# Block 0's x in two parts, conv weights decoded in PSUM, and new engine letters for the first blocks of a fused dynamic convolution and gated FFN

## The chip, the cores and the metric

One core of a Trainium2 chip runs the kernel. The metric is the device time of one execution in microseconds; lower is better. The engines are PE (matrix multiply), DVE (VectorE), ACT (ScalarE), POOL (GpSimd) and SP (which here only issues transfers). Each works through its own queue in order and waits for the others by semaphores.

## What is computed

Two layers, one after the other, on 4 sequences of 4160 tokens with 192 channels. The first is a dynamic convolution: per token and head (8 heads of 24 channels) a softmax over 7 weights, and the weighted sum of the last 7 rows of x. The second is a feed-forward layer with a convolution of width 3 over time as its gate.

```python
w = softmax(weight_gen)                     # over 7 taps, per token and head
out[s] = sum_k w[s, h, k] * x[s - 6 + k]    # rows before the sequence are zero
h = np.maximum(out @ w_in, 0.0)             # 192 -> 1024
conv_out[s] = sum_k conv_w[k] * h[s - 1 + k]
y = (h * sigmoid(conv_out)) @ w_out         # 1024 -> 192
```

## The kernel before

**Tiling.** The 16640 tokens are cut into 128 segments of 130 tokens, one per partition. A block is 4 tokens of every segment, so 512 tokens; with two rows of overlap there are 33 blocks. x lives in a ring of 24 rows per partition (`ring`). Block 0 also needs a halo, the seven rows in front of each segment: these are loaded from the neighbour's segment.

**Attention of block q** (`head`). Seven taps, one for each k (`tap`, L292), each multiply 4 rows of x with their softmax weights into a piece of `px` or `py`, 128 x 768 elements. A letter in `PLAN` says for each tap whether VectorE ("V") or GpSimd ("G") does it. Blocks 0 to 2 are of kind "a": PE adds the seven pieces while it transposes them (L327), in two parts of 128 and 64 channels, into the PSUM banks `tp` and `ops`; that is 14 groups of four transposes. Later blocks add most pieces by accumulating DMAs first. ACT and DVE then split the transposed sum into high and low float32r parts (L338, L343).

**Softmax of group j** (`sm_ops`, one group for block 0, then one for two blocks). Maximum (L239), subtract (L242), exponential on ACT (L245), sum (L248), a small constant (L252, L254), reciprocal (L257), normalise (L264) and, in the first rows of a sequence, an edge product that zeroes taps (L269). The letters in `SMX` say who does the subtract, and who the last two.

**FFN of block j** (`unit`, `out_tiles`). For each of the 8 slices f of 128 hidden channels PE runs five matmuls into one of 5 PSUM banks z (`mm1`, L359); ACT does the relu (L365) and the middle conv tap (L369), DVE the two outer ones (L376), ACT the tanh (L383), DVE the gate product (`gmul`, L392), which frees the bank. Then PE makes four output tiles (`mm2`, L405), ACT copies them out (L414) and SP stores them. A unit needs its weight slice (`w_rdy`), a bank and the split block.

**Weight decoding** (`dec`). All weights arrive as raw words and are decoded in six steps: on ACT the exponent shift (L133) and the low half (L136), then clamp (L140), shift (L143), sign (L146) and join (L151). In mode "S" the work lies in SBUF: the letters say who clamps and joins, shift and sign are DVE's. In mode "P" it lies in the single PSUM bank `dps`, all four steps are DVE's whatever the letters say, and the chunks follow each other through that bank. A chunk of w_in then gets a high part (ACT, L595) and a low part (L600). `CH` lists the chunks: "m" for channels 0 to 127, "f" for the other 64 folded in two, whose parts are then spread by DMA (L614). The conv weights are decoded by the same steps, transposed by PE (L567) into the `tp` bank and copied to `cw` by ACT (L572); the first transposes of block 0 on `tp`, and all relus of block 0, wait for that copy.

**Order.** The kernel lists all work as tasks with engine, estimated duration and dependences, places them by a list scheduler, and emits each engine's queue in that order. The list is ranked by `now`: softmaxes of the first groups and weight decoding first (-9), attention of block q at q + `TO`, its transposes at q + `FO`, the units of block j at j to j + 7/8, in block 0 in the order `FORD`, its output tiles from j + `WO_` on. `arrive(t)` stands for data expected at t. A task of kind "VK" is DVE work that the scheduler lets hold POOL too; before the next POOL task after one it emits a pair of memsets on a small tile, `tok` (L874 on DVE, L875 on POOL), so POOL waits there until DVE has got that far. In the other direction nothing is enforced.

**Loads.** SP issues, in this order: the fold chunk 0:256 (two transfers), x rows 0 to 2, the halo (112 and 15 partitions), weights of group 1, x of blocks 1 and 2, the other chunks of w_in, weights of groups 2 and 3. ACT issues the weights of group 0, the chunk m 0:256 and the conv weights.

## Time and profile before

| | us |
|---|---|
| median of 3 runs | 713.72 (713.22 to 714.27) |
| profiled execution, time | 713.11 |
| its span in the profile | 711.40 |
| PE busy | 690.1 (97%) |
| DVE busy | 625.6 (88%) |
| ACT busy | 549.9 (77%) |
| POOL busy | 510.5 (72%) |

The span runs from the first instruction to the last; 1.7 us of the time lie around it. Busy time is the union of the spans of an engine's instructions; the ends of matmuls are modelled. The share over the whole span hides the stages: nearly all of PE's idle time lies in the first 29 us and in the last 3 us.

### The profile page before, as it was taken

Reading aid. Unit: us, or ns where it says so; the run is one execution under the profiler, and the core shown is the slowest. Engines: PE = TensorE matmul, PEld = TensorE weight load, DVE = VectorE, ACT = ScalarE, POOL = GpSimd, SP = SyncE. Lnnn points to the kernel's source line nnn. Section 1 sums busy time; section 2 is a strip of 40 time slices with the busy share of each in tenths; the row PEclk is TensorE's granted clock in tenths of the full one; section 3 lists DMA queues with packets and bytes.
Section 4 is the critical chain, followed back from the end, with each engine's and each line's share of the span. In section 5 each row is a group of like instructions: output and inputs, shape, how many; then the busy total and the mean of one; then the engine's idle time right before and its main releaser. Section 6 shows DMA issues by size and latency. Waiting matters only on the chain.

```text
span 711.4 us, 10938 instructions
## 1 busy us (share of the span) xinstructions
PE 690.1 (97%) x3809; PEld 629.0 (88%) x3809; DVE 625.6 (88%) x975; ACT 549.9 (77%) x1049; POOL 510.5 (72%) x392
## 2 busy tenths in 40 slices
PE   1899999999999999999999999999999999999998
PEld 1788999999999999999999999999999999999998
DVE  6999998989999998998898988988898888888981
ACT  2588888887888787878787877878778778787881
POOL 3998999999987778887777778877767788630000
PEclk9999999999999999999999999999999999999999
DMA  7736999898989688798888788788879886781211
GB/s 226 212 98 166 215 217 225 211 236 197 229 186 211 166 208 200 167 209 189 193 193 200 190 181 202 184 200 193 188 181 200 178 183 163 163 181 68 76 43 45
DMA packets 70787, 127.59 MB, mean 179 GB/s; under 512 B 5046, under 2 KB 42573, under 8 KB 70732
## 3 DMA queue, kind: packets, MB, share of 16 engines
q0 software_dynamic: 20160, 58.99, 46.9%
q1 hardware_dynamic: 50090, 67.51, 29.3%
q8 instruction: 30, 0.49, 0.3%
q10 hardware_dynamic: 482, 0.40, 0.2%
q14 instruction: 25, 0.20, 0.1%
HBM read 20.51 MB, written 12.78 MB: 47 GB/s over the span
## 4 chain that ended last, share of the span: by engine, by line
PE 96%; DMA 2%; DVE 1%; POOL 0%; SPq 0%; ACT 0%; issue 0%; POOLq 0%
PE ops L405 47%; PE z L359 43%; PE tp L327 5%; DMA ring<-in_x_dram 1%; PE ops L327 1%; PE z L405 1%; DMA stage<-in_moe_w_in_dram 1%; DVE py L292 0%; POOL px L292 0%; POOL py L292 0%; SPq L437 0%; DVE r L257 0%; DVE m L248 0%; DVE w L242 0%; DVE px L292 0%
## 5 line engine op out<-in xcount | busy, mean ns | idle before, releaser
L376 DVE SCALAR_TENSOR_TENSOR z<-h,cw,z 128x512 f32<-128x512 f32 (+1 forms) x528 | 379.3, 741 | 25.7 <-ACT z L369 21.3
L405 PE MATMUL ops<-wo,g 128*128 128x192 f32 x2048 | 353.1, 326 | 0.0
L405 PEld LDWEIGHTS ops<-wo,g 128*128 128x128 f32 x2048 | 338.9, 190 | 10.0
L359 PE MATMUL z<-H,wi 128*128 128x512 f32 x1056 | 303.6, 409 | 1.0 <-ACT wi L595 1.0
L292 POOL TENSOR_TENSOR px<-ring,w 128x768 f32<-128x768 f32 (+2 forms) x146 | 231.9, 1702 | 79.6 <-PE tp L327 75.3
L359 PEld LDWEIGHTS z<-H,wi 128*128 128x128 f32 x1056 | 191.1, 189 | 32.5 <-ACT wi L595 1.4
L392 DVE SCALAR_TENSOR_TENSOR g<-z,h 128x512 f32<-128x512 f32 (+1 forms) x264 | 178.3, 679 | 22.3 <-ACT z L383 14.6
L383 ACT ACTIVATE z<-z 128x512 f32<-128x512 f32 (+1 forms) x264 | 151.3, 573 | 45.2 <-DVE z L376 43.4
L369 ACT ACTIVATE z<-h,cw 128x512 f32<-128x512 f32 (+1 forms) x264 | 179.9, 682 | 5.7
L365 ACT ACTIVATE h<-z 128x512 f32<-128x512 f32 x264 | 155.7, 590 | 29.1 <-PE z L359 27.8
L292 POOL TENSOR_TENSOR py<-ring,w 128x768 f32<-128x768 f32 (+2 forms) x108 | 162.8, 1813 | 2.2 <-DMA px<-py 2.2
L359 PE MATMUL z<-L,wi 128*128 128x512 f32 x264 | 103.1, 391 | 0.0
L322 POOL TENSOR_TENSOR px<-px 128x768 f32<-128x768 f32 x30 | 68.0, 2265 | 6.1 <-DMA px<-px 6.1
L414 ACT ACTIVATE o<-ops 128x192 f32<-128x192 f32 x128 | 41.9, 328 | 24.0 <-PE ops L405 22.8
L359 PEld LDWEIGHTS z<-L,wi 128*128 128x128 f32 x264 | 49.6, 188 | 11.2
L338 ACT ACTIVATE H<-tp 128x512 fp32r<-128x512 f32 (+1 forms) x63 | 37.3, 593 | 21.5 <-PE tp L327 20.1
L327 PE MATMUL tp<-ident,px 128*128 128x128 f32 (+1 forms) x288 | 44.5, 279 | 2.7 <-POOL px L292 1.9
L315 POOL DMA_DIRECT2D px<-py x30 | 41.3, 1377 | 7.2 <-POOL py L292 7.2
L318 POOL DMA_DIRECT2D px<-px x30 | 36.3, 1211 | 13.2 <-DMA px<-py 12.0
L327 PEld LDWEIGHTS tp<-ident,px 128*128 128x128 f32 (+1 forms) x288 | 34.6, 132 | 9.5 <-POOL px L292 2.4
L343 DVE TENSOR_TENSOR L<-tp,H 128x512 fp32r<-128x512 f32 x33 | 22.7, 687 | 6.9 <-ACT H L338 6.9
L343 DVE TENSOR_TENSOR H<-tp,H 64x512 fp32r<-64x512 f32 x30 | 20.5, 684 | 6.7 <-ACT H L338 5.9
(67 smaller groups left out, 180.4 us busy)
## 6 DMA issues: line engine op xcount, KB each, us to landing
px<-py POOLq DMA_DIRECT2D x30, 1152.0 KB, 10.2
h<-h SPq DMA_DIRECT2D x128, 256.0 KB, 4.4
px<-px POOLq DMA_DIRECT2D x30, 768.0 KB, 6.6
ring<-in_x_dram SPq DMA_DIRECT2D x31, 384.0 KB, 6.0
out_dram<-o SPq DMA_DIRECT2D x31, 384.0 KB, 2.4
w<-in_weight_gen_dram SPq DMA_DIRECT2D x15, 224.0 KB, 6.5
r_out<-in_moe_w_out_dram SPq DMA_DIRECT2D x4, 384.0 KB, 5.6
wi<-scr SPq DMA_DIRECT2D x8, 128.0 KB, 5.2
```

Source lines behind the costliest of these rows:

```text
L292: eng.tensor_tensor(out=dst[:, a:b, :].rearrange("p s (h g) -> p s h g", g=GRP), in0=ring[:, p:p + n, :].rearrange("p s (h g) -> p s h g", ...
L322: nc.gpsimd.tensor_tensor(out=a, in0=a, in1=b, op=ALU.add)
L327: nc.tensor.matmul(dst[0:D2 if part else P, c * P:(c + 1) * P], lhsT=src[:, c, part * P:part * D2 + P], rhs=ident, is_transpose=True, star ...
L343: nc.vector.tensor_tensor(out=H[D2:P, :] if part else h_t[q, "L1"], in0=tp[r, :], in1=H[r, :].bitcast(F32), op=ALU.subtract)
L359: nc.tensor.matmul(out=z, lhsT=w[:, fs], rhs=h_t[j, nm], start=(i == 0), stop=(i == len(terms) - 1))
L365: nc.scalar.activation(out=hrow(f, 2, R), in_=z_t[j, f], func=ACTF.Relu)
L369: nc.scalar.activation(out=z_t[j, f][:, :no * P], in_=hrow(f, cc, no), func=ACTF.Copy, scale=cw[:, NF + f:NF + f + 1])
L376: nc.vector.scalar_tensor_tensor(out=z, in0=hrow(f, cc + d, no), scalar=cw[:, k * NF + f:k * NF + f + 1], in1=z, op0=ALU.mult, op1=ALU.add,)
L383: nc.scalar.activation(out=z, in_=z, func=ACTF.Tanh, scale=0.5)
L392: nc.vector.scalar_tensor_tensor(out=g_of(j, f), in0=z_t[j, f][:, :no * P], scalar=1.0, in1=hrow(f, cc, no), op0=ALU.add, op1=ALU.mult)
L405: nc.tensor.matmul(out=ps[:, 0:D], lhsT=g_of(j, f)[:, i * P:(i + 1) * P], rhs=wo[:, f, :], start=(f == 0), stop=(f == NF - 1),)
L414: nc.scalar.activation(out=o_t[j][:, i, :], in_=ps[:, 0:D], func=ACTF.Copy, scale=0.5)
```

## The change

- `load_x` no longer loads the halo. A new `load_halo` does, called twice: rows -4 to -1 before x rows 0 to 2, and rows -7 to -5 after them. The zeroing of the first segment's halo stays ahead of both.
- `TORD`: block 0's taps are made, and added by PE, in the order 6, 5, 4, 3, 2, 1, 0; taps 3 to 6 of block 0 depend on the first part of x alone (expected at 8.6), the others on all of it (10.3). Later blocks keep their order.
- The conv weights are decoded in mode "P", and that work is listed behind the first two chunks of w_in; their expected arrival is 10.5 instead of 8.9.
- Engines: block 1's tap 2 goes to DVE. Group 0's subtract, normalise and edge product go from DVE to POOL; group 1's normalise and edge product go to POOL; group 2's subtract goes to DVE. The chunk m 256:512 is decoded in mode "S" with the clamp on POOL.
- The expected arrival of chunk m 0:256 becomes 10.4 (8.7); `TO`, `FO` and `WO_` are -2.55, -0.5 and 1.42; `FORD` is changed; the mask product of the last group goes from DVE to ACT.

```diff
 PLAN = (
     ("a", "GVGGVGG"),
-    ("a", "GGGGGGG"),
+    ("a", "GGVGGGG"),
     ("a", "GGGGGGG"),
 )
-SMX = ("VV", "VV", "GG", "GG")
+SMX = ("GG", "VG", "VG", "GG")
-TO = -2.7
-FO = -0.35
-WO_ = 1.62
+TO = -2.55
+FO = -0.5
+WO_ = 1.42
+TORD = ((6, 5, 4, 3, 2, 1, 0), (0, 1, 2, 4, 5, 6, 3))
 CH = (
     ("f", 0, 256, 5.2, "VGP", "G"),
-    ("m", 0, 256, 8.7, "VVP", "G"),
+    ("m", 0, 256, 10.4, "GVP", "V"),
     ("f", 256, 512, 17.0, "GVP", "V"),
-    ("m", 256, 512, 16.0, "VVP", "G"),
-    ("m", 512, 1024, 18.0, "VVP", "V"),
+    ("m", 256, 512, 16.0, "GVS", "V"),
+    ("m", 512, 1024, 18.0, "VVP", "G"),
 )
-FORD = (0, 3, 1, 5, 2, 4, 7, 6)
+FORD = (0, 2, 1, 3, 5, 4, 7, 6)
-WOE = ("VVP", "VVP", "GVP", "VGP")
+WOE = ("VVP", "VGP", "GGP", "VGP")
...
+    def load_halo(r0, r1):
+        p = slot(r0)
+        for p0, np_ in ((16, 112), (1, 15)):
+            nc.sync.dma_start(
+                out=ring[p0:p0 + np_, p:p + r1 - r0, :].rearrange("p s d -> p (s d)"),
+                in_=seg(xf, D, p0, np_, r0, r1 - r0),
+            )
...
         def keep():
             r = m(1)[:, (n - 1) * HEADS:, :]
-            V.tensor_scalar(out=r, in0=r, scalar1=mask[:, 1:2], scalar2=None, op0=ALU.mult)
+            nc.scalar.activation(out=r, in_=r, func=ACTF.Copy, scale=mask[:, 1:2])
...
-        load_x(-TAPS, 3)
+        G.memset(ring[0:1, slot(-TAPS):slot(0), :], 0.0)
+        load_halo(-4, 0)
+        load_x(0, 3)
+        load_halo(-TAPS, -4)
...
-        x_t_ = {0: arrive(10.3), 1: arrive(13.5), 2: arrive(15.0)}
+        x_t_ = {-1: arrive(8.6), 0: arrive(10.3), 1: arrive(13.5), 2: arrive(15.0)}
...
-        c0 = dec(cw_raw.bitcast(I32), r_cw, temps[0][0:3 * NF, 0:P], temps[1][0:3 * NF, 0:P], arrive(8.9), [], "VVS")[0]
+        def conv_weights():
+            banks = {}
+            c0 = dec(cw_raw.bitcast(I32), r_cw, temps[0][0:3 * NF, 0:P], temps[1][0:3 * NF, 0:P], arrive(10.5), [], "VVP")[0]
...
         for c, (kind, a, b, t, eng, wle) in enumerate(CH):
+            if c == 2:
+                c2 = conv_weights()
...
-            for i, k in ((0, 0), (1, 1), (2, 2), (4, 4), (5, 5), (6, 6), (3, 3)):
+            for i in TORD[q > 0]:
+                k = i
...
-                p_ = task("VK" if e == "V" else e, d_, [sm[group(q)], x_t_[q]] + (xdep if i < 4 else ydep),
+                p_ = task("VK" if e == "V" else e, d_, [sm[group(q)], x_t_[q if q or k < 3 else -1]] + (xdep if i < 4 else ydep),
...
-                out_ = [(i, prod[i]) for i in (0, 1, 2, 4, 5, 6, 3)]
+                out_ = [(i, prod[i]) for i in TORD[q > 0]]
```

## Rows read from the trace of the kernel before

**Rows 1.** Busy time by stage: stretch, length, busy of each engine, clock, DMA
```profile
14.36:28.93 14.57, 10.84 (x63) 9.05 (x64) 13.17 (x28) 5.28 (x14) 10.93 (x12) 1.00 0.66 171
28.93:56.97 28.04, 28.03 (x176) 23.90 (x176) 27.74 (x59) 24.70 (x51) 27.72 (x20) 1.00 0.44 146
85.20:105.61 20.41, 20.41 (x113) 18.72 (x113) 20.02 (x31) 16.99 (x33) 19.00 (x15) 1.00 0.93 213
123.44:143.89 20.45, 20.45 (x113) 18.68 (x113) 19.76 (x31) 16.68 (x32) 18.59 (x14) 1.00 0.92 212
```

**Rows 2.** Chain of work, issues (start, length), landings (last column), SP's wait
```profile
2.10 7.00 DMA ring<-in_x_dram
...
2.72 0.44 SPq L174 DMA_DIRECT2D ring<-in_x_dram  x1
...
ring<-in_x_dram SPq DMA_DIRECT2D x1, 588.0 KB, 7.6
...
2.60 0.36 ACTq L434 DMA_DIRECT2D stage<-in_moe_w_in_dram  x1
...
stage<-in_moe_w_in_dram ACTq DMA_DIRECT2D x1, 256.0 KB, 6.7
...
SPq L199 <- DMA ring<-in_x_dram: 3.6, 1, 3.6
```

**Rows 3.** DVE in order of time: start, length, line, operation, idle before
```profile
7.79 0.35 DVE L257 RECIPROCAL r<-m 128x32 f32<-128x32 f32 x1
...
10.88 0.21 DVE L140 TENSOR_SCALAR h<-h 24x128 f32<-24x128 f32 x1 [2.04 <-ACT h L133]
11.03 0.37 DVE L269 TENSOR_TENSOR w<-w,edge 128x224 f32<-128x224 f32 x1
...
13.03 1.18 DVE L151 CUSTOM_DVE_ANT_0 h<-h 24x256 uint16<-24x256 uint16 x1
...
15.35 1.02 DVE L242 TENSOR_TENSOR w<-w,m 128x448 f32<-128x448 f32 x1
16.30 0.94 DVE L292 TENSOR_TENSOR px<-ring,w 128x768 f32<-128x768 f32 x1
...
18.56 1.70 DVE L292 TENSOR_TENSOR py<-ring,w 128x768 f32<-128x768 f32 x1
20.19 0.61 DVE L264 TENSOR_TENSOR w<-w,r 128x448 f32<-128x448 f32 x1
...
21.99 0.67 DVE L269 TENSOR_TENSOR w<-w,edge 128x168 f32<-128x168 f32 x1
...
24.36 0.43 DVE L140 TENSOR_SCALAR dps<-dps 128x256 f32<-128x256 f32 x1 [0.47 <-ACT dps L133]
```

**Rows 4.** POOL in order of time, same columns
```profile
12.53 1.54 POOL L292 TENSOR_TENSOR px<-ring,w 128x768 f32<-128x768 f32 x1
...
17.85 0.10 POOL L875 MEMSET tok<- 128x1 f32 x1 [1.96 <-DVE tok L874]
...
20.87 0.10 POOL L875 MEMSET tok<- 128x1 f32 x1 [1.42 <-DVE tok L874]
...
22.79 1.54 POOL L292 TENSOR_TENSOR px<-ring,w 128x768 f32<-128x768 f32 x1
24.28 0.97 POOL L242 TENSOR_TENSOR w<-w,m 128x448 f32<-128x448 f32 x1
```

**Rows 5.** ACT in order of time, the fold chunk 256:512
```profile
17.97 0.39 ACT L133 ACTIVATE dps<-stage 128x256 f32<-128x256 f32 x1
```

**Rows 6.** End of the ramp: PE and DVE in order of time; PE's wait
```profile
50.90 0.55 DVE L151 CUSTOM_DVE_ANT_0 wo<-dps,scr 128x768 uint16<-128x768 uint16 x1
...
56.97 1.21 PE L359 MATMUL z<-H,wi 128*128 128x512 f32 x4
...
59.41 5.36 PE L405 MATMUL ops<-wo,g 128*128 128x192 f32 x32
...
PEld z L359 <- DVE g L392: 0.3, 1, 0.3
```

More of the change, by code (lines that the diff above doesn't have):

```diff
@@ L162, in slot @@
         return (r + TAPS + 2) % RING
+    def load_halo(r0, r1):
[5 more added lines that the diff above has]
+            )
     def load_x(r0, r1):
-        a, b = max(r0, 0), min(r1, SEG)
+        a, b = r0, min(r1, SEG)
         p = slot(a)
-        if r0 < 0:
-            nc.gpsimd.memset(ring[0:1, slot(r0):p, :], 0.0)
         nc.sync.dma_start(
@@ L171, in load_x @@
         )
-        if r0 < 0:
-            for p0, np_ in ((16, 112), (1, 15)):
-                nc.sync.dma_start(
-                    out=ring[p0:p0 + np_, slot(r0):p, :].rearrange("p s d -> p (s d)"),
-                    in_=seg(xf, D, p0, np_, r0, -r0),
-                )
         if r1 > SEG:
@@ L275, in sm_ops @@
              ("A" if j else "VK", 0.16 if j else 0.1, eps), ("V", 0.07 + 0.05 * n, rec)]
-            + ([("VK", 0.1, keep)] if j == NG - 1 else [])
+            + ([("A", 0.2, keep)] if j == NG - 1 else [])
             + [(ek[1], ed[1], norm)]
@@ L540, in bits @@
                     if 0 not in hold:
-                        hold[0] = ps_d.tile([P, W], F32, tag="dps", name="dps").bitcast(I32)[:, 0:N]
+                        hold[0] = ps_d.tile([P, W], F32, tag="dps", name="dps").bitcast(I32)[0:t1.shape[0], 0:N]
                     return hold[0]
@@ L561, in dec, with cw_fin @@
             return task("VK" if je == "V" else "G", vec(N, 0) if je == "V" else pool(N), [t_, i1], st[5]), bits
-        c0 = dec(cw_raw.bitcast(I32), r_cw, temps[0][0:3 * NF, 0:P], temps[1][0:3 * NF, 0:P], arrive(8.9), [], "VVS")[0]
-        def cw_fin():
-            cp = ps_t.tile([P, 4 * P], F32, tag="tp", name="tp")
-            nc.tensor.transpose(cp[:, 0:3 * NF], cw_raw, ident[0:3 * NF, 0:3 * NF])
-            banks["cw"] = cp
-        banks = {}
-        c1 = task("P", 0.1, [c0], cw_fin)
-        c2 = task("A", 0.1, [c1], lambda: nc.scalar.activation(out=cw, in_=banks["cw"][:, 0:3 * NF], func=ACTF.Copy))
+        def conv_weights():
+            banks = {}
+            c0 = dec(cw_raw.bitcast(I32), r_cw, temps[0][0:3 * NF, 0:P], temps[1][0:3 * NF, 0:P], arrive(10.5), [], "VVP")[0]
+            def cw_fin():
+                cp = ps_t.tile([P, 4 * P], F32, tag="tp", name="tp")
+                nc.tensor.transpose(cp[:, 0:3 * NF], cw_raw, ident[0:3 * NF, 0:3 * NF])
+                banks["cw"] = cp
+            c1 = task("P", 0.1, [c0], cw_fin)
+            return task("A", 0.1, [c1], lambda: nc.scalar.activation(out=cw, in_=banks["cw"][:, 0:3 * NF], func=ACTF.Copy))
         spreads = []
```

## The prediction, made before the change was run

> **What bounds the kernel now.** I read the busy time by stage first, then the waits of the matmul engine, then the first 60 us in order of time. From 28.93 us on PE has no idle time: 28.03 of 28.04 us up to 56.97, and 20.45 of 20.45 us in a block of the middle, at a granted clock of 1.00 [rows 1]. Such a block asks PE for 8 units of mm1 (L359), 4 output tiles (L405) and 2 transposes. So the end is fixed by when the dense stretch of PE begins, plus work that the change leaves as it is. Before 28.93 PE is busy 10.84 of 14.57 us, and before 14.36 not at all. What the change can win lies here; its reordering of the later blocks can win or lose only a little.
>
> What holds PE back until 28.93 is block 0: its seven taps feed the transposes, these the split, and this the first mm1. The first tap starts on POOL at 12.53 and the last POOL tap at 22.79 [rows 4], ending at 24.33; from there to 28.93 is 4.6 us of transposes, splits and the first unit. The five POOL taps last 5 x 1.54 = 7.7 us of the 11.8 us from 12.53 to 24.33. The other 4.1 us are token waits for VectorE, the longest 1.96 and 1.42 us [rows 4]. The start at 12.53 is late for a reason that is easy to miss: DVE had the reciprocals of group 0 at 8.14 and then stood still 2.04 us, because the first convolution-weight operation (L140 on h) was next in its queue and its data had not arrived; the edge product that frees the first tap (L269) stood behind it and started at 11.03 [rows 3].
>
> From 28.93 to 56.97 DVE is nearly as full as PE, 27.74 of 28.04 us [rows 1], and at 56.97 a unit of mm1 starts just after a wait of 0.3 us for a z bank that DVE had to free [rows 6]. So DVE is a second bound in the ramp, and a head start of PE is kept only as far as DVE follows or PE has something else to do.
>
> **First tap.** Two edits act on it. The conv-weight decode moves behind the decode of the main weights, so nothing late stands in front of group 0 on DVE; and subtract, normalise and edge product of group 0 move to POOL, idle then. On POOL a 448-element subtract took 0.97 us [rows 4], so one of 224 elements costs between half of that, 0.49, and 0.97; I take 0.55, near the half. The subtract costs 0 to 0.6 us more than on DVE; I take none, as the exponential stood behind other ACT work anyway. After 8.14: a token of about 0.2, normalise 0.55, edge product 0.55, so the first tap at about 9.5; with both ends, 9.3 to 10.7. Is x there? Today x rows 0 to 2 land at 9.10 and the 588 KB halo, issued at 2.72, at 10.32 [rows 2]. Taps 6 to 3 need only rows -4 to 2, and these now go first; they land by 9.1 if they behave as today's first piece and by 10.32 if as today's halo. I take the first, as the bytes ahead of them are fewer than those that had landed by 10.32. First tap: 12.53 - 9.5 = 3.0 us earlier, bounds 1.8 to 3.2. The x load has two more issues on SP of about 0.45 us each ([rows 2] show one). Behind them are the loads of group 1's weights, x of blocks 1 and 2 and the rest of w_in. SP now waits 3.6 us before that first load until x has landed [rows 2], which covers the 0.9 us; without that cover they come 0.9 us later, and group 1 with them.
>
> **Block 0's taps.** POOL gets group 1's normalise (0.97 us), its edge product (168 elements, 0.37 by the same rate) and the clamp of chunk m 256:512 (none in the trace; between 0.1 and 0.55, taken 0.3): 1.6 us. In return the token wait of 1.42 us goes, which stood for DVE doing that normalise. The 1.96 us wait, behind group 1's subtract, a DVE tap and the sum, may stay or go; I let it stay, as these three remain. So the span of 11.8 us grows by 0.2, between 1.8 less and 1.6 more, and the last tap ends 2.8 us earlier (3.0 - 0.2), bounds 0.2 to 5.0. The order 6 to 0 costs nothing by itself: 14 groups of transposes either way. Their first on the tp bank still waits for the conv weights, whose join ends at 14.21 today [rows 3]. Behind the chunk m 0:256 (landing at 9.3 to 10.3, then some seven steps of 0.43) four short steps end at about 14 to 15; that is hidden, as by then only three taps are done.
>
> **VectorE's account up to 56.97.** Saved: group 0's edge product 0.37, group 1's normalise 0.61 and edge product 0.67, the clamp 0.43: 2.1 us [rows 3]. The conv join, 1.18 us in SBUF, falls to perhaps 0.4 in the PSUM bank, and the shift and sign of the chunk that leaves PSUM cost 0 to 0.4 less: 0 to 1.2 together. Added: group 2's subtract, 0.61 (a free normalise of that size) to 1.02 (group 1's subtract), and one tap of block 1, 0.94 to 1.70 [rows 3]: 1.6 to 2.7. Net saving -0.6 to +1.7; I take 0.5. The 2.04 us stall becomes usable once the main chunk m 0:256 has landed, issued at 2.60 and 6.7 us on its way [rows 2], 9.3: work could start about 0.5 later, at 9.8 instead of 10.88; I take 0.6 of 0 to 1.1. By DVE alone PE's dense work may come 1.1 us earlier (-0.6 to 2.8).
>
> **What PE keeps.** The chain gives 2.8, DVE 1.1. Between them lies filler: the two output tiles of block 0 run at 59.41 for 5.4 us, though the last w_out decode ends at 51.45 [rows 6]. With the weight 1.42 for 1.62 such tiles rank ahead of later units, so PE can fill a lag of DVE with them. I take 2.4, nearer the chain. **Nothing** comes from FORD (units 2 and 3 need the same two chunks), from the mask product moved to ACT in the last group (0.1 to 0.2 us under PE's continuous work), and from the letters of WOE, since a decode in PSUM uses V whatever they say. TO, FO and WO_ reorder the steady blocks. I see two orders there, 20.41 and 20.45 us a block [rows 1]; over 29 blocks that is at most 1.2 us to either side, and I take 0.
>
> Sum against the profiled execution's own 713.11 us (span 711.40): 713.11 - 2.4 = 710.7. The median of the runs, 713.72, lies 0.6 above it, so the time to expect is 713.72 - 2.4 = **711.3**.
>
> One rule of the Trainium skill speaks against the change. The trace shows a DVE tap of 0.94 us and one, at 18.56, of 1.70 [rows 3]; beside this one POOL ran a tap of 1.54 from its token of 17.85 on [rows 4], to about 19.5, so the DVE tap ended 0.8 after POOL's. The Trainium skill (SBUF — State Buffer, Who interferes with whom) says that a VectorE instruction with two SBUF inputs and a GpSimd one that reads SBUF exclude each other: whoever comes second waits for the whole of the other. The trace agrees. By that rule block 1's new tap and group 2's subtract could each lose up to a POOL tap's 1.54 us; that is an estimate, and it would turn the 2.4 into a loss of 0.7 (case B, its far end).
>
> **Rivals.** (A) *The chain gives more*: the 1.96 us wait goes too and DVE keeps up through filler; 4 us less, 709.7. For: POOL had 4.1 us of waits. Against: DVE is full. (B) *DVE is the bound, or x lands with the halo*: only the 1.1 us of DVE's account stay (or 12.53 - 10.7 = 1.8 us at the first tap, less about 0.8 for POOL's new work): 712.7. If DVE's two new instructions are each held for a whole POOL tap, 2 x 1.54 = 3.1 us, nothing stays: 2.4 - 3.1, so 714.4. For: [rows 1, 6] show DVE full and a bank awaited. Against: 5.4 us of filler. In this case the change in effect moves a wait from POOL to the z banks. (C) *POOL stalls on the new clamp, slower*: the clamp of m 256:512 stands in POOL's queue among block 0's taps and waits for ACT's first step on that chunk. ACT's step for the fold chunk before it starts at 17.97 today [rows 5], so this one comes at about 18.4 and the clamp at 18.9. If POOL reaches it after four taps, 9.5 + 6.2 = 15.7, it stands 3.2 us, and the taps, tokens and group 1's products behind it too. Chain: 3.0 - 3.2 - 1.6 (new POOL work, no wait saved) = 1.8 later: 715.5. It is slower than before from a stall of about 1.4 us on. For: the queue is in order and the chunk is late. Against: the chunk needs no bank now, so ACT may take it earlier. (D) *The later blocks lose* what the front gains, through the new order: 2.4 - 1.2 leaves 712.5, inside case B's time.
>
> **How the numbers follow.** A difference within 0.2% (1.43 us, 712.3 to 715.1) is about what a measurement of this kernel can't tell from none. Forecast 711.3 (709.9 to 712.3): 0.55. A: 0.13. B and D: 0.18. C: 0.14. Faster 0.55 + 0.13 = 0.68, same 0.18, slower 0.14. The range leaves out C and the lowest part of A, and reaches 2.4 below the forecast (order 1.2, a wait of 1.2 more gone) and 2.7 above it (most of B): 708.9 to 714.0.
>
> **What would show it.** Right: first POOL tap at 9.3 to 10, no DVE wait of 2 us before 11; last tap of block 0 at about 21.3; PE dense from about 26.5 with no idle time after; output tiles of block 0 before the last units of block 1; blocks of 20.4 us; the last output tile 2.4 us earlier. Wrong: PE waits for gmul between 45 and 75 (B), a POOL wait of over 1 us at the clamp (C), a block period other than 20.41 to 20.45 (D), or transposes held by the conv weights' copy beyond 16 us.

## The result, and the profile after

The changed kernel is slower: 724.69 us as the median of 6 runs (724.44 to 727.4), against 714.32 (713.22 to 718.08) for the kernel before on the same chips. The ratio is 1.0148, with a 95% interval from 1.0120 to 1.0176, so 10.4 us were lost where 2.4 were forecast as won. The profiled execution took 724.73 us with a span of 723.0. In the changed kernel's code every line of the functions below stands one line later (L360 for L359, L344 for L343, L328 for L327, L406 for L405, L293 for L292); where the spacing edit of e3 is in, it is two lines.

I read the busy time by stage first, in the same four stretches as [rows 1]. The columns are stretch, length, busy time (with instructions) of PE, PE's weight loads, DVE, ACT and POOL, then granted clock, DMA share and GB/s.

```profile
14.36:28.93 14.57, 8.98 (x54) 7.43 (x53) 11.29 (x25) 4.91 (x14) 8.83 (x12) 0.88 0.83 216
28.93:56.97 28.04, 28.04 (x181) 24.84 (x182) 27.69 (x60) 23.89 (x50) 26.47 (x19) 1.00 0.37 125
85.20:105.61 20.41, 19.68 (x108) 17.65 (x107) 18.29 (x29) 15.47 (x31) 19.78 (x15) 1.00 0.86 193
123.44:143.89 20.45, 20.45 (x114) 18.70 (x113) 19.76 (x31) 16.99 (x35) 19.86 (x15) 1.00 0.96 214
```

Three things differ from [rows 1]. The front is emptier, not fuller: PE 8.98 instead of 10.84 us (another 1.45 us of its work now lie before 14.36, where it had none), DVE 11.29 instead of 13.17, POOL 8.83 instead of 10.93. The clock's column is no help in this first stretch: it says 1.00 for the kernel before, but four of its transposes took about 1.06 us each time up to 20.8 and 0.60 from 22.8 on, so it too ran its first transposes at half speed. The ramp up to 56.97 is as full as it was. And a block in the middle has holes: 19.68 of 20.41 us, where the kernel before had none. The page's chain of work that ended last tells the same. In the kernel before it was PE for 96% of the span; now it is this:

```profile
PE 42%; POOL 23%; DMA 19%; DVE 10%; issue 3%; ACT 2%; SPq 1%; POOLq 0%; DVEq 0%
```

The waits of PE (who waits on what, us in total, times, the longest) name the two places:

```profile
PE ops L328 <- POOL py L293: 12.9, 2, 12.5
PE tp L328 <- DVE L L344: 5.6, 6, 2.1
PE tp L328 <- DVE px L293: 3.7, 1, 3.7
PE tp L328 <- POOL px L323: 2.0, 1, 2.0
PE tp L328 <- ACT cw L578: 1.0, 1, 1.0
PE z L360 <- DVE H L344: 1.0, 1, 1.0
```

The first line is the start, before anything is there. The third is in the front: block 0's transposes waited 3.7 us for a tap on DVE. The second and the sixth lie mostly in the late blocks: transposes into the `tp` bank waited for DVE's split six times (once of these at 28.88), and a unit once.

Where in the span was the time lost? I take the start of the same output tile in both traces and subtract: of block 0 the first, of a later block the third, since by these two the same work of PE has gone before in both kernels (the new ranks move others by a unit within their block). The first is at 59.41 in the kernel before [rows 6] and at 59.78 in the changed one, so 0.37 us later; the last matmul ends 11.29 us later. So 10.92 of 11.29 us were lost behind the first output tile, where the prediction had put nothing. Idle time of PE makes 7.69 us of it: 1.95 at block 3's first transposes (79.24), and 5.74 in six later waits. Another 2.2 us are a lower clock after one of them: block 11's output tile (made beside the transposes of block 13) is 5.35 us further behind than block 10's, and only 1.02 + 2.13 = 3.15 us of that are waits. About 1 us is left without a place of its own.

**The late blocks.** The transposes of a block come in two parts, 128 and 64 channels, and from block 3 on both go into the one `tp` bank. The second part has to wait until DVE has split the first. What stands between them in PE's queue is therefore the time that DVE has. Here is one such block (block 7) in the timeline of PE of the kernel before (start, length, line, operation, tiles, shape, count, idle time before and its releaser), and then of the changed kernel:

```profile
155.79 0.60 PE L327 MATMUL tp<-ident,px 128*128 128x128 f32 x4
156.15 1.17 PE L359 MATMUL z<-H,wi 128*128 128x512 f32 x4
...
157.39 2.76 PE L405 MATMUL ops<-wo,g 128*128 128x192 f32 x16
159.99 0.60 PE L327 MATMUL tp<-ident,px 128*64 128x128 f32 x4
```

```profile
157.13 0.60 PE L328 MATMUL tp<-ident,px 128*128 128x128 f32 x4
157.49 1.18 PE L360 MATMUL z<-H,wi 128*128 128x512 f32 x4
...
158.73 1.08 PE L360 MATMUL z<-H,wi 128*128 128x512 f32 x4
159.65 0.39 PE L360 MATMUL z<-L,wi 128*128 128x512 f32 x1
160.66 0.63 PE L328 MATMUL tp<-ident,px 128*64 128x128 f32 x4 [0.62 <-DVE L L344]
```

Before, one unit and one output tile stood between the parts (156.15 to 159.99, 3.8 us); now it is two units (157.49 to 160.04, 2.6 us). The split itself is not slow. These are the splits of the first part on DVE, before and changed:

```profile
158.53 0.68 DVE L343 TENSOR_TENSOR L<-tp,H 128x512 fp32r<-128x512 f32 x1
```

```profile
159.97 0.63 DVE L344 TENSOR_TENSOR L<-tp,H 128x512 fp32r<-128x512 f32 x1
```

In the kernel before it ended at 159.21 and the second part started 0.78 us later; in the changed kernel it ended at 160.60 and the second part started 0.06 us later, which means that it had waited. The kernel's queues show how regular this is. Counted over blocks 3 to 32:

```
work of PE between the two parts of a block's transposes (blocks 3 to 32)
before     30 x one unit and one output tile
changed    23 x two units, 6 x two units and one output tile, 1 x one output tile
```

With the old spacing the second part started 2.0 to 2.24 us after the split in 25 of these 30 blocks; with the new one it starts at most 0.81 us after it in 24 of them. What DVE may be late without PE feeling it has shrunk by about 1.4 us. The largest waits come from one delay of DVE, in blocks 12 and 13. First DVE in order of time:

```profile
271.08 0.62 DVE L240 TENSOR_REDUCE m<-w 128x64 f32<-128x448 f32 x1 [4.79 <-DMA w<-in_weight_gen_dram]
...
286.21 0.69 DVE L344 TENSOR_TENSOR L<-tp,H 128x512 fp32r<-128x512 f32 x1
```

Then PE in the same stretch:

```profile
272.47 0.73 PE L360 MATMUL z<-H,wi 128*128 128x512 f32 x2 [1.02 <-DVE H L344]
...
279.33 2.76 PE L406 MATMUL ops<-wo,g 128*128 128x192 f32 x16
...
286.96 0.98 PE L328 MATMUL tp<-ident,px 128*64 128x128 f32 x4 [2.13 <-DVE L L344]
287.74 2.76 PE L406 MATMUL ops<-wo,g 128*128 128x192 f32 x8
```

And the busy times and the clock by stage (columns as above):

```profile
272.00:286.00 14.00, 12.36 (x64) 10.72 (x64) 13.12 (x20) 10.30 (x20) 13.45 (x10) 1.00 0.60 147
286.00:296.00 10.00, 9.04 (x43) 8.52 (x44) 8.61 (x14) 7.93 (x16) 6.00 (x5) 0.83 0.83 181
```

DVE stood 4.79 us with a maximum at the head of its queue, whose softmax weights had not landed; the units' convolution steps and the split stood behind it. PE lost 1.02 us at once, and at the next block's split, with DVE still behind, 2.13 us. After that wait the granted clock was 0.83 in ten microseconds (0.50 from 288 to 290, which is the lower level, 1.2 GHz), and eight matmuls of an output tile took the 2.76 us that sixteen take at the full clock.

**The front.** These lines of DVE answer [rows 3]:

```profile
9.66 0.96 DVE L293 TENSOR_TENSOR py<-ring,w 128x768 f32<-128x768 f32 x1 [0.62 <-POOL w L270]
...
14.21 1.69 DVE L243 TENSOR_TENSOR w<-w,m 128x448 f32<-128x448 f32 x1
...
20.73 0.61 DVE L240 TENSOR_REDUCE m<-w 128x64 f32<-128x448 f32 x1
21.38 0.62 DVE L243 TENSOR_TENSOR w<-w,m 128x448 f32<-128x448 f32 x1
...
22.64 0.62 DVE L249 TENSOR_REDUCE m<-w 128x64 f32<-128x448 f32 x1 [0.30 <-ACT w L246]
23.18 1.32 DVE L293 TENSOR_TENSOR px<-ring,w 128x768 f32<-128x768 f32 x1
```

And these of POOL [rows 4]:

```profile
10.70 0.10 POOL L884 MEMSET tok<- 128x1 f32 x1 [1.08 <-DMA ring<-in_x_dram]
10.88 3.04 POOL L293 TENSOR_TENSOR py<-ring,w 128x768 f32<-128x768 f32 x2
...
16.08 3.04 POOL L293 TENSOR_TENSOR px<-ring,w 128x768 f32<-128x768 f32 x2
...
25.03 0.10 POOL L884 MEMSET tok<- 128x1 f32 x1 [1.35 <-DVE tok L883]
25.10 0.39 POOL L141 TENSOR_SCALAR scr<-scr 128x256 f32<-128x256 f32 x1
27.57 0.10 POOL L884 MEMSET tok<- 128x1 f32 x1 [2.08 <-DVE tok L883]
```

POOL has its five taps of block 0 done at 19.12, 5.2 us earlier than before. But block 0 has two more taps, on DVE, and the second of them runs only from 23.18 to 24.50, behind the whole softmax of group 2. PE waited for it, and the clock was down afterwards (0.50 from 24.5 to 27; four transposes in 1.12 us, later 0.63):

```profile
24.55 1.12 PE L328 MATMUL tp<-ident,px 128*128 128x128 f32 x4 [3.69 <-DVE px L293]
...
28.88 0.63 PE L328 MATMUL tp<-ident,px 128*128 128x128 f32 x4 [0.86 <-DVE L L344]
```

So the last tap of block 0 ended at 24.50, where it had ended at 24.33. Yet the first unit is 2.05 us later (29.27 for 27.22). PE adds the taps in the order 6 to 0, so tap 0, long done on POOL, had to stand behind the late tap 1: four groups of transposes were left at 24.50 (24.55 to 28.02, mostly at half clock), where the kernel before had two left (24.38 to 25.47).

### The profile page after: what moved, and what is told of

Same layout as the page of the kernel before. It is cut to its first block, busy times and chain, and to the rows that moved or that the text cites. A ratio compares the mean times of both kernels' runs of the same rounds, so it can differ in the third digit from the quotient of the medians.

```text
span 723.0 us, 10934 instructions
## 1 busy us (share of the span) xinstructions
PE 693.2 (96%) x3809; PEld 630.2 (87%) x3809; DVE 626.6 (87%) x971; ACT 550.7 (76%) x1050; POOL 512.1 (71%) x397
## 4 chain that ended last, share of the span: by engine, by line
PE 42%; POOL 23%; DMA 19%; DVE 10%; issue 3%; ACT 2%; SPq 1%; POOLq 0%; DVEq 0%
PE ops L406 21%; PE z L360 17%; DMA px<-py 14%; POOL py L293 10%; POOL px L293 7%; DVE z L377 6%; DMA w<-in_weight_gen_dram 3%; PE tp L328 2%; POOL px L323 2%; POOL px L319 2%; DVE g L393 2%; ACT z L384 1%; DMA stage<-in_moe_w_in_dram 1%; DMA ring<-in_x_dram 1%; PE z L406 1%
## 5 line engine op out<-in xcount | busy, mean ns | idle before, releaser
L406 PE MATMUL ops<-wo,g 128*128 128x192 f32 x2048 | 354.5, 327 | 0.0
L406 PEld LDWEIGHTS ops<-wo,g 128*128 128x128 f32 x2048 | 338.6, 190 | 8.1 <-DVE H L344 0.4
L360 PE MATMUL z<-H,wi 128*128 128x512 f32 x1056 | 300.8, 406 | 1.0 <-DVE H L344 1.0
L293 POOL TENSOR_TENSOR px<-ring,w 128x768 f32<-128x768 f32 (+1 forms) x145 | 230.6, 1727 | 52.3 <-PE tp L328 52.2
L360 PEld LDWEIGHTS z<-H,wi 128*128 128x128 f32 x1056 | 193.0, 188 | 35.3 <-DVE H L344 1.5
L293 POOL TENSOR_TENSOR py<-ring,w 128x768 f32<-128x768 f32 (+2 forms) x108 | 163.9, 1803 | 0.9 <-DMA px<-py 0.8
L360 PE MATMUL z<-L,wi 128*128 128x512 f32 x264 | 102.8, 389 | 0.0
L360 PEld LDWEIGHTS z<-L,wi 128*128 128x128 f32 x264 | 49.6, 188 | 10.9
L328 PE MATMUL tp<-ident,px 128*128 128x128 f32 (+1 forms) x288 | 44.6, 279 | 11.3 <-DVE L L344 5.6
L328 PEld LDWEIGHTS tp<-ident,px 128*128 128x128 f32 (+1 forms) x288 | 33.9, 131 | 18.7 <-DVE L L344 7.5
L339 ACT ACTIVATE H<-tp 128x512 fp32r<-128x512 f32 (+1 forms) x63 | 37.2, 591 | 11.0 <-PE tp L328 10.3
L344 DVE TENSOR_TENSOR L<-tp,H 128x512 fp32r<-128x512 f32 x33 | 22.7, 689 | 5.8 <-ACT H L339 4.9
L265 POOL TENSOR_TENSOR w<-w,r 128x448 f32<-128x448 f32 (+1 forms) x17 | 22.8, 1342 | 0.5 <-DVE r L258 0.5
## 6 DMA issues: line engine op xcount, KB each, us to landing
px<-py POOLq DMA_DIRECT2D x30, 1152.0 KB, 10.3
```

Source lines behind the costliest of these rows:

```text
L293: eng.tensor_tensor(out=dst[:, a:b, :].rearrange("p s (h g) -> p s h g", g=GRP), in0=ring[:, p:p + n, :].rearrange("p s (h g) -> p s h g", ...
L328: nc.tensor.matmul(dst[0:D2 if part else P, c * P:(c + 1) * P], lhsT=src[:, c, part * P:part * D2 + P], rhs=ident, is_transpose=True, star ...
L360: nc.tensor.matmul(out=z, lhsT=w[:, fs], rhs=h_t[j, nm], start=(i == 0), stop=(i == len(terms) - 1))
L406: nc.tensor.matmul(out=ps[:, 0:D], lhsT=g_of(j, f)[:, i * P:(i + 1) * P], rhs=wo[:, f, :], start=(f == 0), stop=(f == NF - 1),)
```

## The experiments

All were timed beside the kernel before. Most of the expected totals were missed: e2, e4, e6, e7 and e9 came out slower than any range stated for them, e3 0.2 us faster than its range, e10 and e12 between their two ranges. One table first, so that each can be placed. Columns: start of the first unit of mm1 and of the first output tile (us); how much later than in the kernel before the first output tile of block 0, the third of blocks 3 and 8 and the last matmul are; the idle time of PE from 59 to 100 us and from 100 us on (waits over 0.25 us), all from the profiled executions.

```
                              unit   tile    blk 0  blk 3  blk 8    end   59-100   100-
before                       27.22  59.41     0.00   0.00   0.00   0.00     0.00   0.00
changed                      29.27  59.78     0.37   3.66   4.40  11.29     1.95   5.74
e1_old_ranks                 32.50  65.76     6.35   7.42   9.13   9.13     1.16   1.34
e2_new_ranks_alone           29.42  63.05     3.64   7.46   8.26  15.92     2.39   6.50
e3_part1_later               27.93  58.42    -0.99   2.16   2.09   1.79     2.54   0.00
e4_tap1_on_pool              24.37  62.70     3.29   8.79  13.28  17.04     2.87   8.56
e5_both                      24.62  61.90     2.49   8.39   8.33   8.02     5.18   0.00
e6_loads_conv_alone          35.40  65.81     6.39  10.40  10.40  10.40     2.33   0.63
e7_engines_alone             34.45  67.85     8.44  10.33  10.33  10.33     0.35   0.73
e8_part1_no_clamp            22.81  60.76     1.34   3.34   3.28   2.97     0.60   0.00
e9_no_tap_of_block1_on_dve   22.84  58.41    -1.00   4.57   5.54   5.24     2.46   1.63
e10_front_with_old_ranks     22.97  59.52     0.11   1.95   2.03   2.03     1.65   0.00
e11_fold_of_block3_first     23.37  61.26     1.85   1.86   1.86   1.86     0.00   0.00
e12_subtract_off_dve         24.71  58.41    -1.00   0.50   0.65   0.65     1.02   0.00
```

Up to the first output tile PE has the same work to do in all of them, but for e8, where one unit fewer stands before it; for the same work e8 is 2.5 us late there, not 1.34.

### The ranks, taken back and taken alone

```diff
# e1_old_ranks: the changed kernel with
-TO = -2.55
-FO = -0.5
-WO_ = 1.42
+TO = -2.7
+FO = -0.35
+WO_ = 1.62
# e2_new_ranks_alone: the kernel before with the three new values, and nothing else
```

> The changed kernel with TO, FO and WO_ put back to -2.7, -0.35 and 1.62; everything else of the change stays. After, the changed kernel lost 0.4 us up to the first output tile of block 0 (59.41 to 59.78) and 10.9 us between there and the last one, in waits of PE for block 3's fold at 79, for splits at 101, 161, 272, 287, 412 and 454. Theory R (the three rank numbers made those later waits): they go, about 714.7, within 0.2% of before; PE without waits of over 0.5 us after 30. Theory F (the new front puts POOL behind, and the later waits follow from that whatever the ranks): 722 to 725, the same waits near 79 and 287.

Measured: 722.28 us (720.27 to 722.6), ratio 1.0110 (1.0088 to 1.0132).

> The kernel before with TO, FO and WO_ of the change alone (-2.55, -0.5, 1.42). Theory R: 722 to 726, with waits of PE for folds and splits after 60 us. Theory F: 713 to 715, PE without waits after 30. If both this and the run with old ranks are near 714, it takes the two together, and if both are slow, each alone is enough.

Measured: 727.28 us (725.83 to 728.98), ratio 1.0190 (1.0169 to 1.0212).

The three numbers alone make the kernel before slower by as much as the whole change does, or more. By the table 12.3 of its 15.9 us are lost behind the first output tile, and the spacing of the two parts is two units in 21 blocks. With the old numbers in the changed kernel the spacing is one unit and one tile again, and from block 8 on no time is lost. (The old spacing doesn't absorb every delay: in e1 PE still waited 1.34 us for a split at 189.52.) The total of e1 lies where theory F had put it, but of the two waits that F named the one near 287 is gone, and the one near 79 is down to 0.78 us (81.33). e1 gains only 2.4 us, because its front is 6 us worse: the list puts block 0's tap on DVE at 26.2 instead of 23.2. So the ranks do two things, and undoing them all can't separate these.

### The spacing alone

```diff
# e3_part1_later: the changed kernel with
+PART1 = 0.2
...
-            now[0] = q + FO
...
                 for part in (0, 1):
                     b_ = part if multi else 0
+                    now[0] = q + FO + (0 if multi else PART1 * part)
```

> The changed kernel, all three new ranks kept, but from block 3 on the second part of a block's transposes is ranked 0.2 of a block later. PE's order is that of the changed kernel up to block 7; from there the two parts, which share the one tp bank, have two mm1 units and one output tile between them (about 4.9 us) instead of two units (2.3 us). After, in 23 of 30 blocks only two units stand between, and the second part starts 0.06 to 0.8 us after DVE has freed the bank; before it is one unit and one tile (3.7 us) and mostly 2.24 us. Theory S (this small room is what turns delays of DVE into waits of PE): the waits from 160 us on, with the slow clock after them 7.6 us, go; 716.5 to 718.5. Theory P (POOL and the folds by DMA are too late in the new order, as the chain of waits names them): the waits stay, 723 to 726.

Measured: 716.27 us (715.31 to 716.71), ratio 1.0037 (1.0024 to 1.0049): 8.4 us faster than the changed kernel by the medians. The second part is ranked 0.2 of a block later from block 3 on, which puts two units and one output tile between the parts in 28 of 30 blocks. PE's queue is the same up to block 6. The longest waits of PE in the trace of e3 are:

```profile
PE ops L329 <- POOL py L294: 12.4, 2, 12.0
PE tp L329 <- DVE px L294: 3.6, 1, 3.6
PE tp L329 <- POOL px L324: 1.8, 1, 1.8
PE tp L329 <- DVE L L345: 1.8, 2, 1.0
```

The front's wait for DVE's tap is still 3.6 us and the wait for POOL's fold still 1.8, but no wait is left after 100 us. The delays of DVE are not gone. These are its waits for softmax weights from 100 to 700 us, in the changed kernel and in e3:

```profile
DVE m L240 <- DMA w<-in_weight_gen_dram: 11.3, 5, 4.8
```

```profile
DVE m L241 <- DMA w<-in_weight_gen_dram: 14.4, 8, 2.3
```

In e3 they are more, and they no longer reach PE. That is what tells the cause (too little work between the parts) from the occasion (a late load). One thing it leaves open: the wait of 4.79 us, behind which 5.35 us were lost, has no equal in e3, where the longest is 2.33, so how much of that one the wider spacing would have hidden isn't shown.

The late loads go with the same three numbers. In the seven kernels with the new ranks DVE waited 11.3 to 16.5 us for softmax weights in that stretch; in the seven with the old ones, the kernel before among them, 0 to 2.9. The two pairs that differ by these numbers alone say the same: 0 in the kernel before and 12.6 in e2, 11.3 in the changed kernel and 2.2 in e1. Which of the three numbers does it, and how, wasn't tried.

### The late tap of block 0

```diff
# e4_tap1_on_pool: the changed kernel with block 0's late tap on POOL
-    ("a", "GVGGVGG"),
+    ("a", "GGGGVGG"),
# e5_both: the same, with the later second part of e3
```

> The changed kernel with block 0's tap 1 on POOL instead of DVE. After, POOL had made its five taps of block 0 by 19.1 us, 5.2 earlier than before, and DVE tap 4 by 10.6, but DVE's tap 1 stood behind group 2's subtract and sum and ended at 24.5; PE waited 3.7 us for it. Theory L (this one tap ate the head start): last tap by 21.5, first mm1 at 25.5 to 27 instead of 29.3, and the first output tile 1.5 to 3 us earlier than after's 59.8. Rival M (the decode of the chunk m 256:512, which the second unit needs and which ended at 29.9, or DVE's work up to 57, sets it): the first unit comes earlier, but the first output tile less than 1 us. The waits after 60 us stay or shift, total 720 to 724.

Measured: 731.02 us (727.59 to 732.38), ratio 1.0234 (1.0206 to 1.0262).

> Both edits together: tap 1 of block 0 on POOL, and the second part of the transposes 0.2 later. If S and L hold both: 713.5 to 716.5, and with no wait after 60 us 712. If only S: 716.5 to 718.5. If only L: 720 to 724.

Measured: 721.06 us (719.67 to 721.45), ratio 1.0098 (1.0083 to 1.0114).

The first unit comes 4.9 us earlier (24.37), and it is worth nothing: the next thing that PE needs, block 1's tap on DVE, now runs at 29.3 instead of 26.2, and block 1 and block 3's fold on POOL come later (PE waits 4.0 us for that fold in e5, at 83.34). The front isn't one chain that can be shortened at one end. The pair gives the spacing a second time: e4 and e5 differ by the later second part alone, by 10 us, and PE waits 8.56 us after 100 us in the one and not at all in the other. In e4 a wait of DVE of 2.89 us for weights (401.38) was followed by one of PE of 1.64 (417.26); in e5 one of 3.18 us (274.67) reached PE not at all.

### The parts of the change alone

```diff
# e6_loads_conv_alone: the kernel before with x in two parts, TORD, and the conv weights in the bank
# e7_engines_alone: the kernel before with
-    ("a", "GGGGGGG"),
+    ("a", "GGVGGGG"),
-SMX = ("VV", "VV", "GG", "GG")
+SMX = ("GG", "VG", "VG", "GG")
-    ("m", 256, 512, 16.0, "VVP", "G"),
+    ("m", 256, 512, 16.0, "GVS", "V"),
```

> The kernel before with two parts of the change alone: x of block 0 in two parts with the taps in the order 6 to 0, and the conv weights decoded in the PSUM bank behind the first two chunks (arrivals 8.6, 10.4, 10.5). Engine letters, unit order and ranks are those of before, and its PE order keeps one unit and one tile between the two parts of the transposes. After e3 the changed kernel still loses about 2.8 us to before, in waits of PE for the folds of blocks 3 and 4 on POOL. Theory E (the engine letters put POOL late, the loads and the decode order are a gain as forecast): first tap by 11, no wait of over 0.5 us after 35, 711 to 713. Theory O (any change of the first 25 us re-deals the list's order and loses the tight fit of before, whose block 3 had 0.26 us of room): 715 to 722, with a wait for the fold of block 3.

Measured: 723.83 us (723.16 to 725.75), ratio 1.0141 (1.0123 to 1.0159).

> The kernel before with only the letters of PLAN, SMX and of the chunk m 256:512 of the change (mode S, clamp on POOL); loads, decode order and ranks as before. Theory E: POOL reaches block 1's taps 1.5 us or more later and PE waits for block 3's fold; 715 to 719. Theory O: also slower, so this alone does not tell them apart; a time of 713 to 714 would speak against E.

Measured: 723.52 us (722.62 to 723.69), ratio 1.0128 (1.0111 to 1.0145).

Both keep the old ranks, and both lose their 10.4 us before the output tile of block 3 and nothing after: 6.4 and 8.4 us up to the first output tile, the rest between the two. In e6 the first tap starts at 9.16, earlier than predicted, and block 0's second tap on DVE at 29.23; PE stood 8.75 us in front of it. In e7 two of DVE's taps run only from 25.59 to 27.73, and the first unit starts at 34.45. What PE waited for longest there, beside the start, was not a tap but the conv weights, which this kernel decodes in SBUF as before: 5.96 us for their join, which DVE ran at 23.04, behind group 2's maximum and subtract. So neither part is a gain by itself: each is dealt anew by the list, and in the front of each deal it was a piece of block 0's chain, late in DVE's queue, that PE waited for.

### The clamp, and no tap of block 1 on DVE

```diff
# e8_part1_no_clamp: e3 with
-    ("m", 256, 512, 16.0, "GVS", "V"),
+    ("m", 256, 512, 16.0, "VVP", "G"),
# e9_no_tap_of_block1_on_dve: e8 with
-    ("a", "GGVGGGG"),
+    ("a", "GGGGGGG"),
```

> e3 (the changed kernel with the second part of the transposes later) with the chunk m 256:512 back in the PSUM bank, so without the clamp on POOL and the two token waits of 1.35 and 2.08 us around it at 25.0 and 27.6. If these waits make block 3's fold late (1.95 us at 79 in after, 1.8 in e3): the wait goes and 713 to 714.5. If POOL is late for the normalise and edge product it has taken over, or the list deals a new order: 716 or more.

Measured: 716.95 us (716.45 to 717.63), ratio 1.0041 (1.0026 to 1.0056).

> The kernel with the second part of the transposes later and the clamp of chunk m 256:512 back on DVE in PSUM, and now block 1's seven taps all on POOL, so that one DVE tap is left in the first 30 us, block 0's, early in DVE's queue. It came to 716.95 with block 1's tap on DVE as the last thing in DVE's queue of the ramp, at 39.85 to 41.30, with PE standing 2.5 and 2.2 us at 32 and 41. Theory (the head start of the front is eaten by a DVE tap that the list puts late in DVE's in-order queue): with that tap gone the first mm1 stays at about 23 to 24, both waits go, the first output tile starts 2 to 4 us before the 59.41 of the kernel before, and the total is 711 to 713.5, ahead of the kernel before. Rival (POOL sets the pace: block 1's seventh tap costs it 1.54 us more, and the folded block 3 behind it had 0.26 us to spare in the kernel before): the first tile may come early, but PE stands 2 us or more at block 3's first transposes near 78 us, and the total is 715 to 718. Either way no wait of PE on block 4 or later, since a unit pair and an output tile stand between the two parts of the transposes.

Measured: 719.9 us (718.1 to 720.41), ratio 1.0075 (1.0058 to 1.0093).

In e8 block 0's DVE tap runs at 16.64, and the first unit 6.5 us earlier than in the changed kernel. The head start is then lost twice; DVE and PE in order of time:

```profile
39.85 1.45 DVE L294 TENSOR_TENSOR px<-ring,w 128x768 f32<-128x768 f32 x1
```

```profile
22.81 1.20 PE L361 MATMUL z<-H,wi 128*128 128x512 f32 x4 [0.69 <-ACT H L340]
...
32.26 0.49 PE L361 MATMUL z<-H,wi 128*128 128x512 f32 x1 [2.51 <-ACT wi L604]
...
41.35 0.66 PE L329 MATMUL tp<-ident,px 128*128 128x128 f32 x4 [2.16 <-DVE tok L885]
```

First the weight chunk of the fifth unit isn't decoded, then block 1's tap on DVE is last of all. With that tap on POOL (e9) both waits go and the first output tile comes 1.0 us earlier than before, where the theory had said 2 to 4. The total was worse by 3 us; that is the rival's way, but beyond its 718: PE waited 2.5 us for block 3's fold at 83.18, and there were waits for DVE at 110 and 129. The theory of the late tap holds for the front and doesn't carry the total.

### A version that loses nothing, and what was left

```diff
# e10_front_with_old_ranks: the changed kernel with TO, FO, WO_ of before, and
-    ("a", "GGVGGGG"),
+    ("a", "GGGGGGG"),
-    ("m", 256, 512, 16.0, "GVS", "V"),
+    ("m", 256, 512, 16.0, "VVP", "G"),
# e11_fold_of_block3_first: e10 with
-                    a_ = dadd([a_, prod[3]], 4.4, lambda: fold2(q), 0.775)
+                    a_ = dadd([a_, prod[3]], 4.4 - 1.0 * (q == 3), lambda: fold2(q), 0.775)
# e12_subtract_off_dve: e11 with
-SMX = ("GG", "VG", "VG", "GG")
+SMX = ("GG", "VG", "GG", "GG")
```

> The changed kernel with block 1's taps all on POOL, the clamp of chunk m 256:512 back on DVE in PSUM, and TO, FO and WO_ back at -2.7, -0.35, 1.62; the two parts of the transposes then have one unit and one output tile between them in all 30 later blocks, as in the kernel before. Theory (late DVE tap in the front, and the distance of the parts behind it): no waits of PE from block 4 on, and a first output tile before 59.41 if the list puts no DVE tap late; total 711 to 714. Rival (POOL's pace at blocks 1 to 3 decides): PE stands 2 us or more between 60 and 100 us, total 716 to 720, whatever the front gained.

Measured: 715.59 us (715.04 to 718.89), ratio 1.0035 (1.0017 to 1.0052).

> The kernel with the changed front and the old ranks (715.59), and the second accumulating DMA of block 3 estimated 1.0 us shorter, so that the list puts the fold of block 3 on POOL ahead of group 2's normalise and two cut taps of 3.3 us, which stood before it. There PE stood 1.65 us at 79.70 on that fold, and from there on the kernel was 2.0 us behind the one before, without any further wait. Theory (POOL's order at block 3 is what is left): that wait goes, the rest is as it was, total 713.5 to 714.2, equal to the kernel before within 0.2%. Rival (the ramp's full DVE decides, and the wait at 42.58 of 2.6 us on DVE's split of block 1 only moves): the first output tile later than 59.4 and total 715 or more.

Measured: 717.31 us (715.29 to 718.37), ratio 1.0044 (1.0028 to 1.0060).

> As the run beside it, and group 2's subtract on POOL in place of DVE (0.62 us of DVE's time between 28 and 31, with a token wait of 1.25 us of POOL behind it). Theory (in the ramp DVE is the bound, it was busy 41.8 of 45.4 us from 14 to 59.4): PE's wait for DVE's split of block 1 shrinks by 0.6 us or more and the first output tile comes 0.6 to 1.5 us earlier than in the run beside it; total 712.3 to 713.6. Rival (POOL is the bound too): its 0.97 us more put the taps of blocks 1 and 2 later, the fold of block 3 comes 1 us later than beside it, and the total is 714 to 715.

Measured: 713.89 us (713.04 to 714.82), ratio 1.0002 (0.9993 to 1.0012).

In e10 nothing is lost after 80 us. PE starts its first unit 4.25 us earlier than the kernel before does and has the first output tile 0.11 later. In between it stood 2.64 us for DVE's split of block 1, and ran at half speed for a while after it (four matmuls of a unit in 2.00 us, then in 1.07):

```profile
42.58 1.56 PE L328 MATMUL tp<-ident,px 128*128 128x128 f32 x12 [2.64 <-DVE L L344]
...
45.50 2.00 PE L360 MATMUL z<-H,wi 128*128 128x512 f32 x4
...
47.56 1.07 PE L360 MATMUL z<-H,wi 128*128 128x512 f32 x4
```

e11 takes the fold's wait away, as meant (no wait after 59 us), and the total doesn't fall, as the rival said: the wait for DVE's split is now 3.10 us and the first output tile 1.74 us later. That points to DVE, not POOL, as what holds the ramp. The executions of e11 spread over 3.1 us, and its trace is of the shortest (715.29). e12 moves 0.62 us of work from DVE to POOL: the wait for the split is gone, the first tile is 2.85 us earlier than in e11, and the kernel equals the one before. But 0.62 us of work isn't 2.85 us by itself; the list dealt the ramp anew, and the two effects aren't told apart. What PE still waits for in it, beside the start and the conv weights' copy:

```profile
PE ops L328 <- POOL px L293: 2.0, 1, 2.0
PE z L360 <- DVE g L393: 1.2, 1, 1.2
PE tp L328 <- POOL px L323: 1.0, 2, 0.6
```

The first of these is in the front (24.33), the second just before the first output tile (57.15), the third at blocks 3 and 4. Of the 1.65 us that are lost from the first tile on, these fold waits are 1.0; the other 0.65 stand in no wait. No version faster than the kernel before was found.

## Why the prediction was wrong

The miss is 13.4 us by the medians (711.3 forecast, 724.69 measured). In the traces, whose spans lie 11.6 us apart where the medians lie 10.4, 2.8 us stand before the first output tile (2.4 earlier forecast, 0.37 later measured) and 10.9 behind it.

**The step that failed by its size: the later blocks.** "TO, FO and WO_ reorder the steady blocks ... that is at most 1.2 us to either side, and I take 0" is the term that was mis-sized. The time behind the first output tile grew by 10.9 us, and 8.1 of these go with the edit that only widens the spacing of the two parts of the transposes (e3: 10.92 against 2.78 behind the first tile). Rival D had named this loss, and priced it by the same 1.2 us. I had worked the bound out from the two periods that the kernel before shows, 20.41 and 20.45 [rows 1]. But these are two orders that both leave PE full. What an unseen order can cost isn't bounded by them; the nearest row for it would have been how long after DVE's split the second part starts, 2.0 to 2.24 us in 25 of 30 blocks. The block period itself was predicted right (20.45 of 20.45 in the undisturbed stretch): the loss sits at seven places, not in every block.

**The step that failed in its reasoning: the last tap of block 0.** I predicted its end 2.8 us earlier (0.2 to 5.0) and measured 0.17 later. The parts were right or better: the first tap ran at 9.66 (predicted 9.5, bounds 9.3 to 10.7), though on DVE; POOL's own first started only at 10.88, behind the token for that tap (the profile puts the wait down to x, which landed at about the same time; in e3 the same wait ended with the token); subtract, normalise and edge product of group 0 took 0.57 to 0.63 each on POOL (predicted 0.55); the token waits of 1.42 and 1.96 us on POOL went both (0.56 is left among its five taps); its five taps ended 5.2 us earlier. But I followed POOL's queue as if it were block 0's, and counted DVE's two taps only as DVE's load. The one that the list had put behind group 2's softmax set the end, and PE's order held tap 0 back behind it. A tap of kind "VK" needs DVE and POOL free in the list, so any change on either engine can throw it elsewhere: 16.6, 23.2, 26.2 and 29.2 in e8, the changed kernel, e1 and e6. One reading in the prediction was off without harm to its sum: DVE didn't stand still from the reciprocals at 8.14 on, it first did a low part of weights and group 0's normalise, and stood from 8.84 to 10.88.

**What PE keeps.** Even where the front worked (e10: first unit 4.25 us earlier than before), the first output tile came at 59.52. Of the predicted 2.4 us no version had more than 1.0 at that tile (e3, e9, e12). This speaks for rival B's first half, that DVE is the bound in the ramp: DVE was waited for at the split (2.64, 3.10) or at the z bank (1.16). The 5.4 us of output tiles that I counted as filler didn't fill these waits.

**Block 3's fold** was in no part of the prediction. In the kernel before POOL finished it 0.26 us before PE wanted it (77.54 and 77.80). In every kernel of the table but that and e11 PE waited for it, 0.3 to 4.0 us.

**VectorE's account.** Its sizes were near: group 2's subtract took 0.62 (0.61 to 1.02), block 1's tap 0.95 (0.94 to 1.70), the conv join in the bank 0.28 instead of 1.18. DVE was less busy in the front than before, and PE was later all the same; the order mattered, not the sum.

**The rival that lost.** C's clamp stood in POOL's queue with a token wait of 1.35 us before it and one of 2.08 behind, but after block 0's taps, not among them. Undoing it changed the whole deal, and the total by less than can be told (e3 and e8: 716.27 and 716.95). Its price by itself stays open.

**The rule on the shared port.** Group 1's subtract on DVE took 1.69 us beside a POOL tap from 13.88 to 15.42, and group 2's, with POOL idle, 0.62. The Trainium skill (SBUF — State Buffer, Who interferes with whom) says that such instructions of the two engines lock each other out. The trace agrees: it cost DVE about 1.1 us at that subtract and 0.4 at the tap of 23.18, much less than the 3.1 us of case B's far end, and it isn't where the time went.

**What stays open.** The changed kernel's front was 1.3 us later in its profiled execution than e3's, though PE's queue is the same up to there; transfers that landed at other times may be the reason, and I didn't take them apart. The late softmax loads go with the new ranks, but how isn't known, and what the wider spacing does with a wait as long as 4.79 us isn't shown. About 1 us of the loss behind the first tile has no place.

## What to carry to other kernels

When one bank is used twice in a row, what stands between the two uses in the matmul engine's queue is the time that the other engines have; count how much of it they leave unused before touching any rank, since a change that costs nothing when all is on time can cost eight microseconds when something isn't. Follow a block's dependences over all engines that make its pieces, not the busiest one's queue. And where a list scheduler deals the queues, undoing one part gives another deal, so compare kernels by the waits in their traces as well as by their totals.

## What the runs showed of the hardware

A short wait of PE in a full stretch can cost more than itself. After a wait of 2.13 us (changed kernel, 286.96) the granted clock fell to 0.83 over ten microseconds, which is partly the lower of the two levels, 1.2 GHz, and cost 2.2 us beside the waits; after 2.64 us (e10) four matmuls of a unit took 2.00 us instead of 1.07. After the wait of 1.95 us at 79.24 they took 1.19, and the clock was 1.00 in the six microseconds behind it. The length of the wait alone doesn't decide it: behind one of 1.88 us (e7, 50.88) the granted clock was 0.72 in six microseconds, behind one of 2.16 us (e8, 41.35) it was 1.00.

A softmax weight load kept DVE standing for 4.79 us in the changed kernel; the longest such wait in the kernel before was 1.6.
